# The first expert quad's products between attention's last steps

## The chip, the cores and the metric

One NeuronCore of a Trainium2 chip. The metric is the device time of one execution in microseconds (us); the kernel before took 2134.57 us (median of three runs, 2134.2 to 2135.18). TensorE is called PE, VectorE DVE, ScalarE ACT, GpSimd POOL; SP issues most DMAs. Each of these takes its instructions in the order in which the kernel issues them, and waits for the others by semaphores.

## The reference

Three layers follow each other, all in fp32:

```python
# 1 attention with random features: q, k, v are (4, 8, 576, 64), omega is (128, 64)
phi(x) = exp(x @ omega.T - |x|^2/2 - rowmax) / sqrt(128)        # x scaled by 64 ** -0.25
kv = phi(k).T @ v;  z = phi(k).sum(rows)
attn = (phi(q) @ kv) / (phi(q) @ z + 1e-6)                      # -> x: (2304, 512)
# 2 eight experts, all of them on every token; P: softmax gate, 8 rounds of row/column scaling
out = sum_e P[:, e] * (relu(x @ w1[e]) @ w2[e])                 # w1: (8, 512, 1024), w2: (8, 1024, 512)
# 3 h = out @ w_in;  y = (h - tanh(h)) @ w_out                  # 512 -> 2048 -> 512
```

## The kernel before, in words

**Attention** (to about 192 us) runs over 16 units, one for each batch and pair of heads. Iteration `i` has five steps `r` = 0 to 4; the loop (L553) runs four iterations past the last unit, and `PLAN` (L546) says which function of which unit comes in which step: in (i, r) = (17, 3) it is `num(14, 0)` and `qpT(15, 0)`. Each step begins with `flush`, which issues the ACT copies and DVE sums that the step before left in `later` and `laterv`. A unit's last stations are `zT` (PE transposes z, then DVE's row sums L472 give `den`, and POOL scales `eq` by it, L485), `qpT` (PE transposes eq into bank `qt`, L351, ACT copies it to `qp`, L502 and L507) and `num` (PE multiplies by `kz` into bank `nd`, L515, ACT copies to `xo`, L527, and SP stores it in the DRAM array `xd`, L528). All PSUM tiles come from a pool of seven banks and one for z. The attention buffers lie in pools `st` and `a2`.

**Experts.** A quad `Q` is 256 rows of the hidden layer of one expert. With tokens in four blocks, a Strassen-like scheme computes it by seven products in place of eight: `quad` (L753) issues product 0 to 7 into three banks `a`, `b`, `e` in the order a0, b1, e2, b3, a4, b5, e6; each is six matmuls (L737), since both operands are split in a high and a low fp32r part. ACT and DVE form `s1`, `u2_`, `v`, `c22` from the banks, then relu'd tiles `h`, again high (L748) and low (L751). The second product (`l2`, L846) multiplies h by w2 into banks `l`, six a quad; those of quad Q are issued within quad Q+1, two behind e2, two behind a4, and so on. In front of quad 0 stands nothing: its products begin when attention's instructions are all issued.

**Preparation** runs by generators that are moved on one step at a time. `weights` (`wprep`) loads raw weights by SP, forms four sums of blocks on POOL for each quad and splits them into seven units `u` (`split`, L82 the high part on ACT, L85 the low part on POOL), and splits w2's slabs into tiles `v`. Its jobs are in the order quad, slab, slab, quad, slab, slab; slabs need the pool `w2p`, which opens only after attention, so in attention it comes to the end of quad 0's seven units and no further. `xops` (`xprep`) loads four blocks of x from `xd`, forms three differences (L231) and splits seven units `x`; in attention's last iterations it is moved on in steps 1 and 3. In quads, `tick` (L908) after each product moves both on, and also `bg`, first the gate: it reloads x as `gx` by ACT's DMA queue, multiplies into banks `lg` and `lgT`, and then scales rows and columns.

**Taking over memory.** The pools of the expert phase (`ppm` for PSUM with five banks `q` and three `l`, `hp` for h, `tp` for the temporaries t) are opened when attention's pools are closed, at L575. A pool opened over the place of a closed one waits for the closed one's last use as a whole.

Of the kernel before, what the change touches and what calls it, by code (L numbers as in the profile page):

```python
# [19 lines left out]
def performer_moe_kernel(ctx, tc, q, k, v, omega, wg, w1, w2, win64, wout64, out):  # L20
    nc = tc.nc
# [27 lines left out]
    NU1, NU2, NV, NX = 16, 6, 7, 8  # L49

# [71 lines left out]
    def weights():  # L122
# [4 lines left out]
        for kind, s in stages:  # L127
# [134 lines left out]

    with ExitStack() as actx, tc.manual_schedule():
        pp = actx.enter_context(tc.tile_pool(name="pp", bufs=7, space=PSUM))
# [8 lines left out]
        qn = [st.tile([P, NCH, 2, D], F32, name=f"qn{i}") for i in range(2)]  # L273
        kn = [st.tile([P, NCH, 2, D], F32, name=f"kn{i}") for i in range(2)]
        vn = [st.tile([P, 2, 2, NCH, D], F32, name=f"vn{i}") for i in range(3)]
# [80 lines left out]
        def norms(u, i):  # L356
# [5 lines left out]
            tmp = a2.tile([P, NCH, 2, D], F32, tag="tmp", name=f"tmp{u}_{i}", bufs=2)  # L362
# [11 lines left out]
        def qkT(u, i):  # L374

            if ("qk", u) not in T:
                T["qk", u] = a2.tile([P, 2, S], F32, tag="qk", name=f"qk{u}")
# [16 lines left out]
        def feat(u, c):  # L394
# [13 lines left out]
            ek = a2.tile([P, 2, M], F32, tag="ek", name=f"ek{u}_{c}", bufs=7)  # L408
# [48 lines left out]
        def zT(u):  # L457

            ps = pp.tile([P, 512], F32, tag="z", name=f"z{u}", bufs=1)
# [85 lines left out]
        NORM, RED, SPL = (0, 1), (2, 4), 4  # L545
        PLAN = [  # L546
# [6 lines left out]
        for i in range(NUN + 4):  # L553
            for r, items in enumerate(PLAN):
# [4 lines left out]
                flush(feat(i, r) if i < NUN else iter(()))  # L559
                for fn, off, arg in items:  # L560
# [14 lines left out]
    ppm = ctx.enter_context(tc.tile_pool(name="ppm", bufs=5, space=PSUM))  # L575
    w2p.append(ctx.enter_context(tc.tile_pool(name="w2p", bufs=NU2)))
    accp = ctx.enter_context(tc.tile_pool(name="accp", bufs=8))
    hp_ = ctx.enter_context(tc.tile_pool(name="hp", bufs=9))
    tp = ctx.enter_context(tc.tile_pool(name="tp", bufs=2))
    phase = ExitStack()  # L580
    ctx.enter_context(tc.manual_schedule())

    def qbank(name):
        return ppm.tile([P, 512], F32, tag="q", name=name)

    def lbank(name):
        return ppm.tile([P, 512], F32, tag="l", name=name, bufs=3)

    def tmp(i, name):
        return tp.tile([P, TB], F32, tag=f"t{i}", name=name)  # L590
# [131 lines left out]
    hs = {}  # L722
    held = []
    acc = {}
    state = {"n1": 0, "x0": 0}

    FIRST = ("A", "B", "E"), ("B", "A"), ("B", "E")

    def htile(name):
        return hp_.tile([P, 2, TB], F32R, tag="h", name=name)  # L730

    def product(ps, i, start, stop, last):
        u, x = u1[state["n1"]], ux[state["x0"] + i]
        m = 0
        for wi, xi in ((0, 0), (0, 1), (1, 0)):
            for c in range(2):
                nc.tensor.matmul(  # L737
                    ps[:, :TB], u[:, wi, c], x[:, xi, c], start=(start and m == 0), stop=(stop and m == 5),
                    skip_group_check=True,
                )  # L740
                m += 1
        spent1.add(state["n1"])
        state["n1"] += 1
        if last:
            spentx.add(state["x0"] + i)

# [304 lines left out]
```

## Time and profile before

| what | us |
|---|---|
| median of three runs | 2134.57 (2134.2 to 2135.18) |
| profiled execution | 2134.26, span 2132.3, mean granted clock 0.996 |
| PE busy | 2105.9 (99% of the span), 10800 matmuls |
| DVE, POOL, ACT busy | 1783.9, 1462.0, 1051.0 |
| tail of attention, 174 to 191.88 | PE busy 14.62 of 17.88 |
| quad 0's products, 191.88 to 199.4 | PE busy 7.51 of 7.52 |
| 199.4 to 212 | PE busy 11.40 of 12.60 |
| 212 to the end | PE busy 1909.15 of 1920.30 |

A share of busy time is a mean over stages; the last four lines cut the span at the places that the change touches. A profile line of an engine gives start and duration in us, source line, operation, tile written and tiles read with their shape, the number of like instructions merged, and in brackets how long the engine stood before it and what ended that wait. The duration of a merged PE line includes the end of its last matmul, beside which the next one already runs. The granted clock is 1.00 at 2.4 GHz and 0.50 at 1.2 GHz.

### The profile page before, as it was taken

To read this page: it belongs to the slowest core of one execution; us is meant where nothing else is said; L and a number is where in the kernel's file an instruction comes from. 1 tells how busy PE (TensorE), PEld (TensorE's weight loads), DVE (VectorE), ACT (ScalarE), POOL (GpSimd) and SP (SyncE) were. 2 spreads that over 40 slices of the span, in tenths; PEclk is the share of its full clock that TensorE was granted. 3 is DMA by queue.
4 is the path that set the end of the run, shared out by engine and by line. 5 is a ranking of instruction groups with operands and counts; after the bars stand their busy time and mean duration, and the time that the engine had idled before them with its cause. 6 is when DMAs were issued, how large, how long until landed. Compare 5 with 4: busy or idle time off the path is not lost.

```text
span 2132.3 us, 33749 instructions
## 1 busy us (share of the span) xinstructions
PE 2105.9 (99%) x10800; PEld 1869.6 (88%) x10800; DVE 1783.9 (84%) x3457; ACT 1051.0 (49%) x2577; POOL 1462.0 (69%) x1981
## 2 busy tenths in 40 slices
PE   8998999999999999999999999999999999999998
PEld 6776899899998898889989899989999899989987
DVE  7885677888897798799888788788875699999997
ACT  6885333333333433333333433333333388778875
POOL 6776677767777777677777867777767546575653
PEclk9999999999999999999999999999999999999999
DMA  6444222323222333232222232323222231222220
GB/s 153 115 129 146 71 80 89 104 82 104 88 89 87 104 92 121 71 105 82 96 95 82 93 105 82 124 82 97 94 66 79 70 104 45 95 84 75 81 74 35
DMA packets 184385, 195.74 MB, mean 92 GB/s; under 512 B 53392, under 2 KB 142992, under 8 KB 184208
## 3 DMA queue, kind: packets, MB, share of 16 engines
q1 hardware_dynamic: 177200, 184.09, 27.4%
q10 hardware_dynamic: 7008, 9.51, 1.3%
q8 instruction: 85, 1.39, 0.3%
q14 instruction: 92, 0.75, 0.1%
HBM read 171.00 MB, written 22.54 MB: 91 GB/s over the span
## 4 chain that ended last, share of the span: by engine, by line
PE 75%; DVE 10%; issue 3%; ACT 2%; POOL 0%; DVEq 0%; DMA 0%; ACTq 0%; POOLq 0%
PE l L846 39%; PE b L737 14%; PE a L737 9%; PE e L737 9%; DVE t L829 3%; PE p L811 2%; DVE t L830 2%; DVE t L822 1%; DVE acc L873 1%; DVE v L85 1%; DVE x L85 1%; ACT t L828 1%; ACT u L82 0%; PE x L895 0%; DVE acc L871 0%
## 5 line engine op out<-in xcount | busy, mean ns | idle before, releaser
L846 PE MATMUL l<-v,h 128*128 128x512 f32 x4320 | 1052.4, 393 | 6.2 <-ACT h L834 3.2
L846 PEld LDWEIGHTS l<-v,h 128*128 128x128 f32 x4320 | 805.4, 188 | 164.4 <-ACT h L834 3.9
L85 POOL TENSOR_TENSOR v<-rs,v 128x256 fp32r<-128x256 f32 x432 | 334.0, 796 | 318.8 <-PE l L846 198.1
L881 DVE SCALAR_TENSOR_TENSOR acc<-l,pt,acc 128x512 f32<-128x512 f32 x516 | 380.3, 744 | 130.1 <-PE l L846 127.3
L85 POOL TENSOR_TENSOR u<-s,u 128x256 fp32r<-128x256 f32 x384 | 297.2, 785 | 81.1 <-ACT u L82 58.5
L737 PE MATMUL b<-x,u 128*128 128x384 f32 x1728 | 351.2, 338 | 0.0
L737 PEld LDWEIGHTS b<-x,u 128*128 128x128 f32 x1728 | 309.4, 188 | 15.1 <-DVE t L764 0.4
L82 ACT CAST u<-s 128x256 fp32r<-128x256 f32 x384 | 154.7, 405 | 282.8 <-POOL s L167 255.3
L737 PE MATMUL a<-x,u 128*128 128x384 f32 x1152 | 234.0, 337 | 0.9 <-ACT xo L527 0.5
L85 POOL TENSOR_TENSOR u<-rq,u 128x256 fp32r<-128x256 f32 x288 | 226.4, 786 | 12.3 <-ACT u L82 8.7
L737 PE MATMUL e<-x,u 128*128 128x384 f32 x1152 | 231.5, 335 | 0.0
L737 PEld LDWEIGHTS a<-x,u 128*128 128x128 f32 x1152 | 205.4, 188 | 10.1 <-ACT xo L527 1.5
L811 PE MATMUL p<-x,u 128*128 128x384 f32 x1152 | 212.9, 338 | 1.3 <-ACT u L82 0.7
L811 PEld LDWEIGHTS p<-x,u 128*128 128x128 f32 x1152 | 203.1, 189 | 7.5 <-POOL u L85 2.3
L737 PEld LDWEIGHTS e<-x,u 128*128 128x128 f32 x1152 | 202.8, 188 | 0.1
L835 POOL TENSOR_TENSOR h<-t,h 128x384 fp32r<-128x384 f32 x96 | 101.4, 1056 | 136.3 <-ACT h L834 129.0
L748 ACT ACTIVATE h<-b 128x384 fp32r<-128x384 f32 x96 | 47.2, 491 | 254.1 <-DVE b L786 253.3
L82 ACT CAST v<-rs 128x512 fp32r<-128x512 f32 x240 | 146.7, 621 | 40.1 <-PE l L846 38.9
L748 ACT ACTIVATE h<-t 128x384 fp32r<-128x384 f32 x96 | 50.4, 526 | 194.9 <-DVE t L773 194.9
L85 POOL TENSOR_TENSOR u<-rqi,u 128x256 fp32r<-128x256 f32 x96 | 93.8, 997 | 41.9 <-ACT u L82 39.6
L82 ACT CAST u<-rq 128x256 fp32r<-128x256 f32 x288 | 117.3, 407 | 1.6 <-ACT xo L897 1.6
L760 ACT COPY t<-a 128x384 f32<-128x384 f32 x96 | 46.1, 480 | 102.2 <-PE a L737 100.2
(141 smaller groups left out, 3071.6 us busy)
## 6 DMA issues: line engine op xcount, KB each, us to landing
rq<-in_moe_w_dram SPq DMA_DIRECT2D x96, 512.0 KB, 3.8
rs<-in_moe_w_dram SPq DMA_DIRECT2D x192, 256.0 KB, 2.8
rqi<-win SPq DMA_DIRECT2D x24, 512.0 KB, 4.6
rs<-wout SPq DMA_DIRECT2D x48, 256.0 KB, 2.8
xt<-xd SPq DMA_DIRECT2D x24, 384.0 KB, 5.9
r<-in_moe_w_in_dram SPq DMA_DIRECT2D x32, 256.0 KB, 3.2
r<-in_moe_w_out_dram SPq DMA_DIRECT2D x32, 256.0 KB, 3.5
xd<-xo SPq DMA_DIRECT2D x32, 144.0 KB, 1.8
```

Of the source, the lines that this page charges most:

```text
L82: nc.scalar.copy(dst[:, 0], src)
L85: eng.tensor_tensor(dst[:, 1, i : i + w], src[:, i : i + w], dst[:, 0, i : i + w].bitcast(F32), ALU.subtract)
L737: nc.tensor.matmul(ps[:, :TB], u[:, wi, c], x[:, xi, c], start=(start and m == 0), stop=(stop and m == 5), skip_group_check=True,)
L748: nc.scalar.activation(h[:, 0], src, AF.Relu)
L760: nc.scalar.copy(s1, A)
L811: nc.tensor.matmul(ps, u1[f + i][:, wi, c], ux[state["x0"] + 2 * t + i][:, xi, c], start=(m == 0), stop=(m == 11))
L822: nc.vector.tensor_tensor(s, u, ps, ALU.mult)
L829: nc.vector.scalar_tensor_tensor(s, gb, B1, s, ALU.add, ALU.mult)
L830: nc.vector.scalar_tensor_tensor(s, ga, A1, s, ALU.add, ALU.mult)
L835: nc.gpsimd.tensor_tensor(lo, s, hi.bitcast(F32), ALU.subtract)
L846: nc.tensor.matmul(ps, hh[f][:, hi, t : t + P], u2[n + f][:, wi], start=(f == 0 and i == 0), stop=(f == len(hh) - 1 and i == 2),)
L881: V.scalar_tensor_tensor(a, ps, p[:, e : e + 1], a, ALU.mult, ALU.add)
```

## The change

1. Product, relu, banks and temporaries (`quad`, `product`, `htile`, `tmp`, `tick`, `need`, `second`, ...) are defined ahead of attention. `quad` becomes a generator `steps` that yields after every product; `quad` runs it through.
2. Step (16, 3) closes attention's PSUM pool and two new pools `fs` and `f2` (with qn, kn, vn, qk, tmp, ek, on the right side of SBUF) and opens `ppm`, `hp` and `tp` there with `reuse_waits="tile"`: each tile then waits for what lay in its own place only. From there attention's banks are the three `l`, and z takes one `q`.
3. `DRAIN` moves quad 0 on by one product in the steps (16, 4), (17, 0) to (17, 4) and (18, 1), each behind that step's own instructions. Each product is followed by a `tick`, which here moves `wprep` on.
4. Two more steps of `xprep`, (16, 4) and (17, 2), so that each x unit is there when its product is issued.
5. Quad 1's weights come second in the jobs, ahead of the first slabs (`lead`), so that its sums and units are made in attention.
6. In the main loop quad 0 takes the ready h tiles.

```diff
+    EARLY = 1
+        lead = [k for k in range(3 * EARLY + 3) if k % 3 == 0]
+        jobs[:] = [jobs[k] for k in lead] + [j for k, j in enumerate(jobs) if k not in lead]
...
+    def open_main():
+        ppm = ctx.enter_context(tc.tile_pool(name="ppm", bufs=5, space=PSUM, reuse_waits="tile"))
+        hp = ctx.enter_context(tc.tile_pool(name="hp", bufs=9, side="right", reuse_waits="tile"))
+        tp = ctx.enter_context(tc.tile_pool(name="tp", bufs=2, side="right", reuse_waits="tile"))
+        return ppm, hp, tp
...
     def product(ps, i, start, stop, last):
+        need(state["n1"], u1, "w")
+        need(state["x0"] + i, ux, "x")
...
-    def quad(Q, last, second):
+    def steps(Q, last, second):
...
         tick()
         turn()
+        yield
...
-        second(2)
+        second(max(2, len(ready) - 6))
...
+    def early():
+        for Q in range(EARLY):
+            hh_early.append((yield from steps(Q, False, second)))
+            yield
...
         def bank(name):
-            return pp.tile([P, 512], F32, tag="b", name=name)
+            return lbank(name) if main else pp.tile([P, 512], F32, tag="b", name=name)
+        fs = units.enter_context(tc.tile_pool(name="fs", bufs=1, side="right"))
+        f2 = units.enter_context(tc.tile_pool(name="f2", bufs=2, side="right"))
...
+        DRAIN = [(0, 0, 0, 0, 1), (1, 1, 1, 1, 1), (0, 1, 0, 0, 0), (0, 0, 0, 0, 0)]
...
+                if (i, r) == (NUN, 3):
+                    units.close()
+                    main.append(open_main())
+                    begin = early()
                 for fn, off, arg in items:
...
                 if (i == 2 or i > 4) and r == SPL:
                     next(wprep, None)
-                if i > 2 * NP + 3 and r in (1, 3):
+                if i > 2 * NP + 3 and (r in (1, 3) or (i, r) in ((NUN, 4), (NUN + 1, 2))):
                     next(xprep, None)
+                if main:
+                    for _ in range(DRAIN[i - NUN][r]):
+                        next(begin, None)
...
-                hh = quad(s * NQ + Q, Q == NQ - 1, second)
-                second(len(ready))
+                if s == 0 and Q < EARLY:
+                    hh = hh_early[Q]
+                else:
...
+                    hh = quad(s * NQ + Q, Q == NQ - 1, second)
+                    second(len(ready))
```

## Rows read from the trace of the kernel before

**Rows 1.** The page's head.

```profile
span 2132.3 us, 33749 instructions
```

**Rows 2.** Busy time by stage: each engine's busy us (instructions), granted clock, DMA share, GB/s.

```profile
174.00:191.88 17.88, 14.62 (x66) 8.34 (x66) 11.70 (x55) 11.22 (x26) 9.84 (x12) 0.71 0.15 50
...
199.40:212.00 12.60, 11.40 (x73) 8.03 (x72) 3.78 (x7) 6.28 (x16) 12.52 (x20) 1.00 1.02 358
212.00:2132.30 1920.30, 1909.15 (x9567) 1717.99 (x9565) 1615.71 (x2750) 897.90 (x2092) 1317.74 (x1661) 1.00 0.27 87
```

**Rows 3.** The same in half microseconds around the fall and rise of the clock.

```profile
181.00:181.50 0.50, 0.50 (x6) 0.50 (x4) 0.41 (x3) 0.07 (x1) 0.00 (x0) 0.56 0.00 0
...
191.00:191.50 0.50, 0.35 (x2) 0.00 (x0) 0.50 (x2) 0.20 (x2) 0.00 (x0) 0.70 0.00 0
```

**Rows 4.** Timeline of PE, tail of attention: start, us, operation, idle before and its releaser.

```profile
176.95 0.71 PE L515 MATMUL nd<-qp,kz 128*64 128x288 f32 x4
...
179.05 0.32 PE L351 MATMUL qt<-ident,eq 112*128 112x112 f32 x1 [0.97 <-POOL eq L485]
...
180.51 0.44 PE L462 MATMUL z<-ident,zr 128*128 128x128 f32 x2
...
187.50 1.41 PE L351 MATMUL qt<-ident,eq 128*128 128x128 f32 x6
...
191.88 1.31 PE L737 MATMUL a<-x,u 128*128 128x384 f32 x6 [0.53 <-ACT xo L527]
...
198.23 1.20 PE L737 MATMUL e<-x,u 128*128 128x384 f32 x6
```

**Rows 5.** Timeline of ACT, same stretch.

```profile
180.03 0.55 ACT L502 COPY qp<-qt 128x464 f32<-128x464 f32 x1 [1.88 <-PE qt L351]
...
191.43 0.40 ACT L527 COPY xo<-nd 128x288 f32<-128x288 f32 x1 [0.30 <-ACT xo L527]
193.74 0.48 ACT L760 COPY t<-a 128x384 f32<-128x384 f32 x1 [1.91 <-DMA xd<-xo]
...
199.44 0.41 ACT L82 CAST u<-s 128x256 fp32r<-128x256 f32 x1 [0.71 <-POOL s L167]
```

**Rows 6.** Timeline of DVE, same stretch.

```profile
177.28 1.25 DVE L231 TENSOR_TENSOR xt<-xt,xt 128x768 f32<-128x768 f32 x1
...
178.85 0.28 DVE L451 TENSOR_SCALAR kz<-kv 128x128 f32<-128x128 f32 x1
...
181.09 0.29 DVE L472 CUSTOM_DVE_ANT_0 jk<-eq,z 128x128 f32<-128x128 f32 x1 [0.71 <-PE z L462]
...
194.33 0.56 DVE L764 TENSOR_TENSOR t<-b,t 128x384 f32<-128x384 f32 x1 [2.37 <-PE b L737]
```

**Rows 7.** Timeline of POOL, two windows.

```profile
166.44 1.77 POOL L485 TENSOR_TENSOR eq<-eq,den 128x256 f32<-128x256 f32 x3 [2.23 <-DVE nm L412]
...
176.53 4.33 POOL L485 TENSOR_TENSOR eq<-eq,den 128x256 f32<-128x256 f32 x5 [6.18 <-DVE den L472]
182.87 3.61 POOL L485 TENSOR_TENSOR eq<-eq,den 128x256 f32<-128x256 f32 x5 [2.02 <-DVE den L472]
186.44 1.95 POOL L85 TENSOR_TENSOR x<-xt,x 128x384 fp32r<-128x384 f32 x2
194.87 2.83 POOL L85 TENSOR_TENSOR v<-rs,v 128x256 fp32r<-128x256 f32 x4 [6.48 <-ACT v L82]
...
200.78 0.72 POOL L85 TENSOR_TENSOR u<-rq,u 128x256 fp32r<-128x256 f32 x1
```

**Rows 8.** Timeline of PE behind quad 0.

```profile
205.79 1.55 PE L846 MATMUL l<-v,h 128*128 128x512 f32 x6
208.13 0.85 PE L623 MATMUL lg<-gx,wgr 128*32 128x384 f32 x8 [0.78 <-DVE acc L871]
```

**Rows 9.** DMA issues from 140 to 216: KB each, median us to landing.

```profile
gx<-xd ACTq DMA_DIRECT2D x12, 384.0 KB, 5.1
...
rq<-in_moe_w_dram SPq DMA_DIRECT2D x2, 512.0 KB, 6.2
```

More of the change, by code (lines that the diff above doesn't have):

```diff
@@ L260, in ready_x, with qbank @@
         return (kind, s) in xdone
+    main, hh_early = [], []
+    def open_main():
[3 more added lines that the diff above has]
+        return ppm, hp, tp
+    def qbank(name):
+        return main[0][0].tile([P, 512], F32, tag="q", name=name)
@@ new lines, in lbank, with tmp, htile, product @@
+    def lbank(name):
+        return main[0][0].tile([P, 512], F32, tag="l", name=name, bufs=3)
+    def tmp(i, name):
+        return main[0][2].tile([P, TB], F32, tag=f"t{i}", name=name)
+    hs = {}
+    held = []
+    acc = {}
+    state = {"n1": 0, "x0": 0}
+    FIRST = ("A", "B", "E"), ("B", "A"), ("B", "E")
+    def htile(name):
+        return main[0][1].tile([P, 2, TB], F32R, tag="h", name=name)
+    def product(ps, i, start, stop, last):
+        need(state["n1"], u1, "w")
+        need(state["x0"] + i, ux, "x")
+        u, x = u1[state["n1"]], ux[state["x0"] + i]
+        m = 0
+        for wi, xi in ((0, 0), (0, 1), (1, 0)):
+            for c in range(2):
+                nc.tensor.matmul(
+                    ps[:, :TB], u[:, wi, c], x[:, xi, c], start=(start and m == 0), stop=(stop and m == 5),
+                    skip_group_check=True,
+                )
+                m += 1
+        spent1.add(state["n1"])
+        state["n1"] += 1
+        if last:
+            spentx.add(state["x0"] + i)
@@ new lines, in performer_moe_kernel, with tick, need @@
+    bg = []
+    pace = [0, 1, False, False]
+    def tick():
+        next(wprep, None)
+        pace[0] += 1
+        if pace[3] or pace[0] % 8 == 0:
+            next(xprep, None)
+        if bg and not pace[2] and (pace[1] == 1 or pace[0] * 12 % 32 < 12):
+            try:
+                next(bg[0])
+            except StopIteration:
+                bg.pop(0)
+    def need(n, have, what):
+        k = 0
+        while n not in have:
+            k += 1
+            assert k < 1000, what
+            next(wprep if what == "w" else xprep)
@@ L263, in performer_moe_kernel, with turn, second @@
+    turned = []
+    def turn():
+        if turned:
+            turned.pop(0)()
+    ready, begun = [], {}
+    def second(n):
+        for _ in range(n):
+            if ready:
+                ready.pop(0)()
+                tick()
+    def early():
+        for Q in range(EARLY):
+            hh_early.append((yield from steps(Q, False, second)))
+            yield
     with ExitStack() as actx, tc.manual_schedule():
-        pp = actx.enter_context(tc.tile_pool(name="pp", bufs=7, space=PSUM))
+        units = ExitStack()
+        pp = units.enter_context(tc.tile_pool(name="pp", bufs=7, space=PSUM))
@@ L272, in performer_moe_kernel @@
         bd = st.tile([P, 2 * M], F32, name="bd")
[L273 to L275 removed]
+        qn = [fs.tile([P, NCH, 2, D], F32, name=f"qn{i}") for i in range(2)]
+        kn = [fs.tile([P, NCH, 2, D], F32, name=f"kn{i}") for i in range(2)]
+        vn = [fs.tile([P, 2, 2, NCH, D], F32, name=f"vn{i}") for i in range(3)]
@@ L719, in convert @@
         converted.append(True)
[L722 to L745, printed above, removed]
@@ L901, in x2 @@
             xdone.add((1, s))
-    bg = []
-    pace = [0, 1, False, True]
-    def tick():
-        next(wprep, None)
-        pace[0] += 1
-        if pace[3] or pace[0] % 8 == 0:
-            next(xprep, None)
-        if bg and not pace[2] and (pace[1] == 1 or pace[0] * 12 % 32 < 12):
-            try:
-                next(bg[0])
-            except StopIteration:
-                bg.pop(0)
-    def need(n, have, what):
-        k = 0
-        while n not in have:
-            k += 1
-            assert k < 1000, what
-            next(wprep if what == "w" else xprep)
-    turned = []
-    def turn():
-        if turned:
-            turned.pop(0)()
     gtp = phase.enter_context(tc.tile_pool(name="gtp", bufs=1))
@@ L935, in performer_moe_kernel @@
     bg.append(gate(gtp))
-    ready, begun = [], {}
-    def second(n):
-        for _ in range(n):
-            if ready:
-                ready.pop(0)()
-                tick()
     n2 = 0
```

136 lines of the change are left out of this document (70 added, 66 removed).

## The prediction, made before the changed kernel ran

> **What bounds the kernel now.** I read first the windows by stage. From 212 us to the end PE is busy 1909 of 1920 us [rows 2]: whatever reaches 212 us earlier arrives earlier by as much, and only the stretch before is worth reading. In the tail of attention (174 to 191.88) PE stands 3.3 us and its mean granted clock is 0.71; from 199.4 to 212 it stands 1.2 us. The half-microsecond windows place the clock: PE stands from 178.1 to 179.05, the clock falls to 1.2 GHz at 181.1 (mean 0.56 in that half) and is back at 2.4 GHz at 191.3 (mean 0.70), 3.8 us into a gapless run of PE from 187.5 [rows 3, 4]. Ten us at half clock are 5 us of PE lost. Last, the timelines of the engines: the tail is a chain DVE sums, POOL scaling of eq, PE transposes (qt), ACT copies, PE products (nd), and PE follows it [rows 4 to 7]. So some 9.5 us (3.3 + 1.2 + 5) are what any reordering could win here at most.
>
> **The change part by part.** The 42 matmuls of quad 0 stand from 191.88 to 199.37 now, 7.49 us, 1.04 to 1.07 a product (I use 1.04, the step from start to start) [rows 4]. They move behind (16,4) to (18,1); nothing is removed. With them move their ACT copies and relus, their DVE sums, the last units of x, and the preparation of quad 1's seven units (ACT cast 0.41, POOL 0.72 each) out of the stretch after 200 us. Everything is issued in the written order, so I lay each engine's queue out from 180.66, where z of the last unit ends; until there nothing on the chain moves (quad 1's four sums on POOL fall into its idle times ahead of eq, 2.2 us and 6.2 us [rows 7]).
>
> *PE's work.* Left of attention: nine groups worth 4.3 us at full clock (four nd at 0.62, which is 0.71 less the overlap with the next; transposes 0.46 a half, 0.22 a rest, estimates at half the durations that the qt rows show at half clock) [rows 4]. With 7 x 1.04 = 7.3 that is 11.6 us. Clock: the fall at 181.1 has its reason before, so it stays. It rose after 3.8 us without a gap; with products behind (14,1) PE is gapless from 180.5, so I put the rise at 184.5, a loss of 1.7 us. Without any wait PE would be through at 180.66 + 11.6 + 1.7 = 194.0.
>
> *What the queues add.* ACT: qp ends 180.6 [rows 5]; then u7's cast 0.41 and x3's 0.79 (twice as many elements as the cast of a u, an estimate), to 181.8, then the copy s1, which waits for product a0 (6 matmuls at half clock, 181.1 to 183.1) and holds everything behind it: 183.7; u8 184.2; xo and qp of unit 14, 185.0; u9 185.4; qp's rest 185.6; x4's cast 186.4. DVE: x3's low part, 181.6 to 182.6 (1.0; 1.25 for the subtraction of the same shape at 177.28, beside POOL), now stands ahead of the last sums, which ran at 181.09 and let POOL begin eq at 182.87: 1.5 us, to 184.1; then u2 (0.56), which waits for b1 until 185.3, and only then the rest of the sums, to 186.9 [rows 6]. POOL: u8 184.2 to 184.95, three eq by 0.72 (3.61 for five) to 187.1, u9 187.8, two eq to 189.2 (the first of them 188.6), and x4's low part, 2 x 0.97 [rows 7], at 190.2 and 191.2. PE: a0 183.1, rest of (14,2) 183.6, b1 185.1, e2 186.2, b3 187.2, nd 187.8; the transposes of unit 15 wait for eq until 188.6 (0.5 lost); a4 can run two matmuls, then waits for the halves of x4 (1.2 and 0.8 lost): 191.8; nd 192.4; the next transposes need a bank of only three that ACT empties behind a4's relu (0.8 lost): 193.7; b5, rest, e6 196.0; two nd 197.2. So quad 0 and attention together end at about 197.2, against 199.37 with quad 0 last: 2.2 gained, 3.3 us of waits eaten.
>
> *What is late next.* The weights of the second product, v0 and v1, are still taken from the space of the pool that closes with attention: the first ACT instruction behind it waited 1.91 us for the last xd<-xo, until 193.66, 2.2 after that xo started [rows 5]. With xo at 197.6 this is 199.8; v0's cast (0.65, the time from ACT's copy to POOL's first half of v) and POOL's halves (2.83 us for the four of v0 and v1 [rows 5, 7]) give v0 at 202.0 and v1 at 203.5. Quad 1's a, b, e need neither (u7 to u13 are ready at 194.9) and run 197.2 to 200.4; then l of quad 0 waits 1.8 for v0 and 0.7 for v1 and ends at 204.3. Before, the same l ended at 207.34 (205.79 + 1.55), with two lg groups and one lgT done as well, 0.78 each (0.85 less overlap) [rows 8], which come later in the new order. 204.3 + 2.3 = 206.6, against 207.3: 0.8 gained. The 0.78 us that lg waited at 208.13 for a bank [rows 8] I count half, 0.4, since lg now starts one step later among the l's. **Sum: -1.2 us.** gx (5.1 to land, issued at about 202) and quad 2's weights (6.2, issued at about 202.5; [rows 9]) then reach their users, lg at 207.7 and quad 2 at some 218, in time. POOL then has v2, v3, four sums and seven units, some 11 us, for quad 2: covered by PE's 14 us of quad 1 and l's; if that cover were gone it would cost the difference, under 3 us.
>
> *Bounds of the terms.* Clock: never fallen (0.8 more gained, because the waits for POOL remain) to low until 191.3 as before, whatever runs (0.8 less; some of its cost lies beside the waits). Waits of 3.3: from 0 (all of it hidden) to 6, if POOL's instructions take what eq took at 176.53, 4.33 for five, rather than 1.77 for three at 166.44 [rows 7]. The stall on v0 and v1, 2.5: from 0 (if quad 1's further products stood there) to 4. The new places: each waits for what lay there last, at most for kz at 179.13 instead of nd's start at 176.95 [rows 4, 6], of which the wait for eq behind it swallows all but 0.9; I take 0, since kz's end is the latest of all and only one of eight places can be its bank.
>
> Of POOL the rows show 0.59 us for an eq at 166.44 and 0.87 at 176.53, where DVE ran a subtraction of two SBUF tiles meanwhile [rows 6, 7]. The Trainium skill, page "SBUF — State Buffer", section "Who interferes with whom", says that DVE with two SBUF inputs and POOL lock each other out. That speaks against the change, which puts three low parts of x on DVE and seven units on POOL into the chain; it is rival C.
>
> **The rivals.**
> A, the chain hides it all: quad 0 fills only what PE lost anyway. Waits of 3.3 gone, quad and attention end at 194.0, the mark comes 3.2 earlier, and the wait of 0.78 goes whole: -1.2 - 3.2 - 0.4 = -4.8, 2129.8. For it: the 3.3 us idle and the slow clock [rows 2]. Against: ACT, DVE and POOL are in order, and each has a piece of quad 0 ahead of a piece of the chain.
> B, the new places wait for the whole closed pools (the change does not do what it says): all first uses wait for 179.13; 0.9 on the chain: -0.3, 2134.3. Against: the pools' last readers are done before the tail's critical part.
> C, POOL is held by DVE: 20% on POOL's times of this stretch (a choice between none and 0.87/0.59 = 1.47), with the queues laid out again, moves the mark by 3.2: +2.0, 2136.6. For: 0.87 against 0.59. Against: 182.87's 0.72, with little of DVE beside it, is in the sum already.
> D, slower, the clock falls a second time: place, the wait for v0 and v1 (200.4 to 203.5), where PE has 0.7 us of work; before the fall at 181.1 its longest stand was 0.97 [rows 4]. Price: as long at half clock as from 181.1 to 191.3, 10 us, 5 lost: +3.8, 2138.4; with a return as quick as the forecast's, +0.6. It decides whether the clock falls in that wait as it fell behind the 0.97. Against: products run densely on both sides, and the clock held through the 1.2 us that PE stood from 199.4 to 212 [rows 2].
>
> **How the numbers follow.** The profiled execution took 2134.26 (span 2132.3 and 2.0 around it) [rows 1], 0.3 below the median 2134.57; the gain is taken off the median: 2134.57 - 1.2 = 2133.4. Chances: forecast 0.42 (its own range 2131.5 to 2135.5), A 0.22, B 0.06, C 0.12, D 0.18. A change under 0.2% (4.3 us, so 2130.3 to 2138.8) cannot be told from none by a measurement of this kernel. Faster: most of A (0.17) and the forecast's lower edge (0.05), 0.22. Slower: the half of D on which C's 2.0 come as well (2140.4; 0.10) and 0.03 of C, 0.13. Same: 0.65. The range leaves out the lower part of A and the upper half of D: 2128.4 to 2138.4.
>
> **What would show it.** In the changed kernel: products a to e among nd and qt from 181 to 196; DVE's sums (L472's successor) starting at about 182.6 instead of 181.09; PE's product a4 waiting for POOL's x; quad 1's first product right behind the last nd; l waiting for POOL's v at some 200 to 203.5; the mark (end of the first l) at 203.5 to 205. Wrong if the last nd comes before 195 (A) or after 199.5 (C), if the clock has a second low stretch after 200 (D), or if the first uses of the new banks wait at 177 (B); and wrong in its frame if PE loses time after 212, where it was gapless.

## The result: slower by 0.66%, most of it after the stretch that the prediction worked out

The changed kernel took 2148.07 us (median of 6 runs, 2142.66 to 2150.24) against 2133.99 for the kernel before beside it (6 runs, 2127.61 to 2135.18): a ratio of 1.0066, 95% interval 1.0049 to 1.0083. The forecast was 2133.4, its range 2128.4 to 2138.4; the time lies above it. The executions of either kernel differ by up to 7.6 us, so medians are compared; a trace shows one execution. The profiled execution took 2148.71, span 2146.9, 14.6 longer than the span before [rows 1].

The windows by stage of the changed kernel, answering to [rows 2] (per engine busy us and instructions; then clock and DMA):

```profile
174.00:200.00 26.00, 21.66 (x113) 16.66 (x115) 18.19 (x63) 15.64 (x40) 15.84 (x19) 0.87 0.11 36
200.00:212.00 12.00, 9.38 (x33) 6.59 (x32) 3.38 (x6) 3.07 (x7) 4.16 (x6) 0.72 0.65 206
212.00:2146.90 1934.90, 1924.27 (x9602) 1716.06 (x9601) 1618.34 (x2750) 900.09 (x2098) 1322.31 (x1668) 1.00 0.27 88
```

After 212 PE stands no more than before (10.6 us against 11.2 [rows 2]), yet the stretch is 14.6 us longer, for 35 matmuls more. The window 500 to 1000 us, in the middle of the long stage, shows why. First the kernel before, then the changed one:

```profile
500.00:1000.00 500.00, 499.92 (x2502) 450.03 (x2501) 428.63 (x749) 191.71 (x460) 364.62 (x479) 1.00 0.30 94
```

```profile
500.00:1000.00 500.00, 499.54 (x2484) 446.25 (x2483) 426.53 (x742) 190.04 (x456) 361.47 (x475) 1.00 0.30 95
```

Same clock (1.00, 2.4 GHz), PE busy throughout, and 18 matmuls fewer. A busy engine can be slow: here the count tells it, and the busy share does not. The first stage's end in PE's timelines (start, duration), before and after:

```profile
1703.79 2.22 PE L846 MATMUL l<-v,h 128*128 128x512 f32 x9
1705.85 2.27 PE L811 MATMUL p<-x,u 128*128 128x384 f32 x12
```

```profile
1717.63 2.96 PE L923 MATMUL l<-v,h 128*128 128x512 f32 x12
1720.44 2.26 PE L888 MATMUL p<-x,u 128*128 128x384 f32 x12
```

The first p is 14.59 later. I set every PE matmul of the changed kernel beside the same one of before. Its lag ("shift") is -0.36 us until 165, +0.91 at 172, -1.43 at the last l of quad 0, the 36th l (before at 226.33), +4.92 at the last l of quad 1, the 72nd (242.81), +14.59 at the first p (1705.85), +14.90 at the last p (2107.04). So some 5 us are lost early, 9.7 evenly between 243 and 1706, nothing after.

The **step** of a matmul is the time from its start to the start of the next on PE; I take the mean between 500 and 1500 us, without the few steps over 250 ns. Of l it is 230.1 ns before and 233.4 after; of a, b and e 175.5, 176.2, 173.5 and 175.0, 175.4, 173.6. The first stage has 3456 l, 1152 a, 1728 b and 1152 e: 3456 x 3.33 - 1152 x 0.48 - 1728 x 0.87 + 1152 x 0.08 = 9.5 us, which is the even loss.

**The early part.** PE's timeline of the changed kernel, for [rows 4, 8]:

```profile
182.02 1.30 PE L300 MATMUL a<-x,u 128*128 128x384 f32 x6
185.45 0.68 PE L300 MATMUL a<-x,u 128*128 128x384 f32 x3
188.34 0.60 PE L300 MATMUL a<-x,u 128*128 128x384 f32 x2
190.49 0.59 PE L300 MATMUL a<-x,u 128*128 128x384 f32 x1 [1.56 <-POOL x L86]
191.45 1.33 PE L300 MATMUL a<-x,u 128*128 128x384 f32 x3 [0.37 <-POOL x L86]
199.84 1.19 PE L676 MATMUL nd<-qp,kz 128*64 128x288 f32 x8
201.24 1.21 PE L300 MATMUL e<-x,u 128*128 128x384 f32 x6
204.38 0.79 PE L923 MATMUL l<-v,h 128*128 128x512 f32 x1 [1.93 <-ACT v L83]
205.87 5.15 PE L923 MATMUL l<-v,h 128*128 128x512 f32 x11 [0.69 <-POOL v L86]
226.08 0.85 PE L781 MATMUL lg<-gx,wgr 128*32 128x384 f32 x8 [0.78 <-DVE acc L948]
```

Quad 0 stands among attention's steps, a4 waits for POOL's x, and l waits for v, as forecast. Not forecast: the three matmuls of a at 185.45. Quad 0's own a are the six at 182.02 and the 2 + 1 + 3 from 188.34, so these three are of quad 1's first product. PE's order is not the written one, unlike what the opening section says: matmuls written behind attention run among its last steps. Whether they are moved when the program is built or by the engine no run here shows. Windows of half a us of the changed kernel, for [rows 3]:

```profile
181.00:181.50 0.50, 0.50 (x5) 0.09 (x2) 0.29 (x1) 0.50 (x2) 0.50 (x1) 1.00 0.00 0
190.50:191.00 0.50, 0.50 (x1) 0.18 (x1) 0.50 (x2) 0.26 (x1) 0.50 (x1) 0.63 0.00 0
197.00:197.50 0.50, 0.50 (x5) 0.50 (x4) 0.00 (x0) 0.00 (x0) 0.00 (x0) 0.54 0.04 9
204.00:204.50 0.50, 0.12 (x1) 0.12 (x1) 0.00 (x0) 0.50 (x2) 0.10 (x1) 0.79 0.00 0
211.00:211.50 0.50, 0.50 (x5) 0.50 (x4) 0.44 (x1) 0.00 (x0) 0.00 (x0) 0.89 1.07 385
```

The clock no longer falls at 181. It falls behind a4's stand, to 197.5, and again behind the stand for v, to 211: two stretches of 6.8 us at 1.2 GHz in place of one of 10.2 [rows 3]. Where it falls differs between executions: in e14's (below), the same order with v moved by 32 bytes, the clock is low around 182 to 185 too, and again later:

```profile
182.00:185.00 3.00, 3.00 (x13) 2.14 (x14) 1.74 (x7) 1.58 (x3) 1.60 (x2) 0.50 0.00 0
196.00:198.00 2.00, 2.00 (x9) 1.90 (x8) 0.09 (x1) 0.83 (x3) 1.60 (x3) 0.50 0.41 136
206.00:212.00 6.00, 5.25 (x12) 3.63 (x12) 0.69 (x1) 0.74 (x2) 3.84 (x6) 0.50 0.94 295
```

What holds ACT and POOL, for [rows 5, 7]:

```profile
203.71 0.62 ACT L83 CAST v<-rs 128x512 fp32r<-128x512 f32 x1 [2.08 <-DMA xd<-xo]
211.77 0.62 ACT L83 CAST v<-rs 128x512 fp32r<-128x512 f32 x1 [5.42 <-DMA rs<-in_moe_w_dram]
213.39 0.52 ACT L311 ACTIVATE h<-t 128x384 fp32r<-128x384 f32 x1 [1.00 <-DVE t L347]
188.73 2.67 POOL L86 TENSOR_TENSOR x<-xt,x 128x384 fp32r<-128x384 f32 x2
```

The fourth slab's cast waited 5.42 us on ACT for its load, and quad 1's relu stood behind it; in the kernel before seven u of quad 1 lie between the second slab and the third. PE did not pay for this wait here. From that cast to the last l of quad 1 it stands 0.88 us, 0.78 of it the wait at 226.08, which the kernel before has at 208.13 [rows 8]:

```profile
211.77:247.73 35.96, 35.08 (x209) 26.55 (x208) 16.18 (x29) 13.75 (x33) 20.69 (x30) 1.00 0.50 162
```

Nor does the rise of the shift from -1.43 to +4.92 say so. At the last l of quad 0 the changed kernel has still to run 24 lg and 24 lgT that the kernel before has done by then, some 5.1 us of PE (0.78 for eight lg, 0.69 for six lgT).

The early loss adds up ahead of 212. From 165 us to the last l of quad 1 PE stands 9.4 us in place of 5.7 (stands over 0.06 us): 1.2 more up to z, 1.93 at a4 and 2.62 at the first l, less 2.2 that the kernel before stands from 183 to 202. At 1.2 GHz half of PE's busy time is lost: 6.3 us in place of 4.5. Together that is 5.4 us more, against 5.3 measured (from -0.36 to +4.92).

### The profile page after: what moved, and what is told of

It reads as the page before. It is cut to its first block, busy times and chain, and to the rows that moved or that the text cites. A ratio compares the mean times of both kernels' runs of the same rounds, so it can differ in the third digit from the quotient of the medians.

```text
span 2146.9 us, 33744 instructions
## 1 busy us (share of the span) xinstructions
PE 2118.3 (99%) x10800; PEld 1867.1 (87%) x10800; DVE 1790.2 (83%) x3457; ACT 1050.7 (49%) x2577; POOL 1462.6 (68%) x1981
## 4 chain that ended last, share of the span: by engine, by line
PE 87%; DVE 8%; issue 2%; ACT 2%; POOL 0%; DMA 0%; SPq 0%; DVEq 0%; ACTq 0%; POOLq 0%
PE l L923 43%; PE b L300 14%; PE a L300 9%; PE e L300 9%; PE p L888 6%; PE pr L561 2%; DVE t L906 1%; PE kv L592 1%; DVE t L907 1%; DVE t L899 1%; PE nd L676 1%; DVE mx L571 1%; DVE acc L950 1%; PE qt L512 1%; DVE jk L633 1%
## 5 line engine op out<-in xcount | busy, mean ns | idle before, releaser
L923 PE MATMUL l<-v,h 128*128 128x512 f32 x4320 | 1070.9, 397 | 8.3 <-ACT h L911 2.6
L86 POOL TENSOR_TENSOR u<-rq,u 128x256 fp32r<-128x256 f32 x288 | 226.6, 787 | 12.0 <-ACT u L83 10.2
L888 PE MATMUL p<-x,u 128*128 128x384 f32 x1152 | 210.8, 337 | 0.4 <-ACT u L83 0.4
```

The source lines that it names most:

```text
L86: eng.tensor_tensor(dst[:, 1, i : i + w], src[:, i : i + w], dst[:, 0, i : i + w].bitcast(F32), ALU.subtract)
L888: nc.tensor.matmul(ps, u1[f + i][:, wi, c], ux[state["x0"] + 2 * t + i][:, xi, c], start=(m == 0), stop=(m == 11))
L923: nc.tensor.matmul(ps, hh[f][:, hi, t : t + P], u2[n + f][:, wi], start=(f == 0 and i == 0), stop=(f == len(hh) - 1 and i == 2),)
```

## The experiments

All times are medians, ratios against the kernel before run beside them, with 95% intervals. "Place" of h or v is where their tiles start in a partition, in bytes past a multiple of 256; the tiles' pitch is a multiple of 256. Before: h 0, v 0. Changed: h 224 (the pool moved to the right side of SBUF), v 0. In both, u and x are at 0.

### Placement or banks: e1, e2, e3, e4

**e1**, the kernel before with h moved:

```diff
+    pad1 = ctx.enter_context(tc.tile_pool(name="pad1", bufs=1)).tile([P, 8], F32, name="pad1")
     hp_ = ctx.enter_context(tc.tile_pool(name="hp", bufs=9))
+    pad2 = ctx.enter_context(tc.tile_pool(name="pad2", bufs=1)).tile([P, 8], F32, name="pad2")
...
```

> The kernel before, with the nine h tiles alone moved up by 32 bytes (a 32-byte tile ahead of them and one behind, so that the temporaries move by 64); h then starts 32 bytes past a multiple of 64, as in the changed kernel. In the changed kernel the steps from one l matmul to the next are 234.2 ns against 230.8 (500 to 1500 us), and 9.5 of the 14.6 us come in evenly over the l matmuls of the first expert stage. T1 (h's address decides, by its offset): l steps of 233.5 to 234.5 ns and 9 to 12 us more than before, 2143 to 2146. T2 (the banks of l decide): 230.8 ns and no change within 1 us. T3 (which h tile is read beside which v, or h lying 22 KB higher, decides): 230.8 ns, no change.

2139.27, 1.0030 [1.0019, 1.0041]. Step of l 233.2; in its trace the shift grows from +0.7 to +9.7 over the first stage. In the trace 32 bytes of padding bring 9.0 of the 9.7 us of even loss into the kernel before. The medians differ by 5.7 us, less than the 9 to 12 of T1; so too in e4 and e7, where the traces show 9 us over the first stage and the medians 6. Why they differ is open. The two pads also move the temporaries t by 64 bytes; e13 against e7 moves h alone.

**e2**, the kernel before with l in banks 0 to 2, as in the changed one:

```diff
+    nc.vector.memset(lbank("l2")[:, :8], 0.0)
```

> The kernel before, with one l bank taken first, so that l lies in banks 0 to 2 and the products in 3 to 7, as in the changed kernel; one small memset is added. T1 (h's offset): 230.8 ns between l matmuls and no change within 1 us. T2 (banks): 233.5 to 234.5 ns, 9 to 12 us slower. T3: no change.

2131.19, 0.9995 [0.9985, 1.0005], step 230.1: the banks make no difference here.

**e3**, the changed kernel with h back at a multiple of 256:

```diff
+    padr = ctx.enter_context(tc.tile_pool(name="padr", bufs=1, side="right")).tile([P, 56], F32, name="padr")
```

> The changed kernel, with a tile of 224 bytes at the right end of SBUF, so that h (and everything else there) starts at a multiple of 256, as in the kernel before; banks, order and pairing as in the changed kernel. T1 (h's offset): l steps back to 229 to 232 ns, 8 to 11 us less than the changed kernel; what stays over the kernel before is the 5 us that the trace shows ahead of 260 us (3.4 us of PE standing, 1.7 us of half clock). T2 (banks) or T3 (place or pairing): 234 ns, as the changed kernel.

2136.5, 1.0014 [1.0005, 1.0023], step 230.1. The shift is -0.3 before the tail, +3.4 at the last l of quad 1 and +4.2 at the first p: the even loss is gone, and most of the early one stays (3.8 of 5.3). With h back in its place the changed kernel lies inside the forecast's range.

**e4**, the changed kernel without quad 0's products in attention (`DRAIN` moves nothing):

```diff
-    EARLY = 1
+    EARLY = 0
```

> The changed kernel with no quad issued early (EARLY = 0): the takeover of banks and buffers in step (16, 3), the two more steps of x and h's new place stay; quad 0 and quad 1's weights come after attention as before. If the early products cost the 5 us ahead of 260 us and the placement the 9.5 us after it: 9 to 11 us slower than before, with the clock falling once at about 181 and PE standing no more than before. If instead the takeover itself costs the early time (waits of its first tiles): 14 us slower, as the whole change.

2139.36, 1.0027 [1.0016, 1.0037], step 233.4: the shift is -0.6 before the tail, -1.6 at the 72nd l and +7.3 at the first p. The early loss belongs to the early products and what goes with them, the even loss to h's place. Nothing is lost by the taking over itself.

### Which place: e5, e6, e7

**e5**, before with h tiles 32 bytes longer, so that nine tiles stand at 0, 32, ... 224, 0; **e6**, before with u moved by 32 bytes; **e7**, before with v moved by 32 bytes:

```diff
-        return hp_.tile([P, 2, TB], F32R, tag="h", name=name)
+        t = hp_.tile([P, 2 * TB + 8], F32R, tag="h", name=name)
+        return t[:, : 2 * TB].rearrange("p (a t) -> p a t", a=2)
```

```diff
+    pads = [ctx.enter_context(tc.tile_pool(name="pad1", bufs=1)).tile([P, 8], F32, name="pad1")]
     w1p = ctx.enter_context(tc.tile_pool(name="w1p", bufs=NU1))
```

```diff
+    pads = [ctx.enter_context(tc.tile_pool(name="pad1", bufs=1)).tile([P, 8], F32, name="pad1")]
     w2p.append(ctx.enter_context(tc.tile_pool(name="w2p", bufs=NU2)))
+    pads.append(ctx.enter_context(tc.tile_pool(name="pad2", bufs=1)).tile([P, 56], F32, name="pad2"))
```

> The kernel before, with each of the nine h tiles 32 bytes longer, so that they start at offsets 0, 32, 64, ... 224, 0 within 256 bytes. T1a (what counts is that h starts at a multiple of 64): steps between l matmuls as before on the tiles at 0, 64, 128, 192, and 233 to 235 ns on the odd ones, mean about 231.5 ns, 4 to 6 us slower. T1b (only multiples of 256 are good): mean about 233 ns, 8 to 10 us slower. T1c (32 past is bad only as the constant offset of all tiles against v): mean at or under 230 ns.

> The kernel before, with the sixteen tiles u (the stationary operand of the products, as h is of l) 32 bytes past a multiple of 64, everything behind them again at a multiple of 256. T1 as a rule for any stationary operand: the products' steps, 172 to 176 ns, grow by 2 to 4 ns; 5184 products of the first stage and 1152 of the second then cost 10 to 20 us. If it is only of l (512 columns, near the limit of what the engine streams): no change of the products and none of the time.

> The kernel before, with the six tiles v (the moving operand of l) 32 bytes past a multiple of 64 and h at a multiple of 256. If the offset matters for the stationary operand only: l steps 230 ns, no change. If it is the relation of h to v that matters (both off would be good, one off bad): 233 to 234 ns, 9 to 11 us slower. If any operand that starts off a multiple of 64 costs: likewise slower, so this run and e5 have to be read together.

e5: 2133.5, 1.0007 [0.9998, 1.0016], step of l 231.3, between the two; 1.1 us more than before, where T1a said 4 to 6. e6: 2131.93, 0.9995 [0.9986, 1.0004]; l 230.4, and a and b faster (174.1 and 173.8 from 175.5 and 176.2). e7: 2138.76, 1.0027 [1.0015, 1.0039], step 233.1. So h is not special: v moved alone costs as much. Moving u, the first product's h, costs nothing, so T1 as a rule for any stationary operand is out.

### Both operands: e9, e13

**e9**, before with h and v (and acc between them) 32 bytes further; **e13** the same with acc back at 0:

```diff
+    pads = [ctx.enter_context(tc.tile_pool(name="pad1", bufs=1)).tile([P, 8], F32, name="pad1")]
     w2p.append(ctx.enter_context(tc.tile_pool(name="w2p", bufs=NU2)))
...
     hp_ = ctx.enter_context(tc.tile_pool(name="hp", bufs=9))
+    pads.append(ctx.enter_context(tc.tile_pool(name="pad2", bufs=1)).tile([P, 56], F32, name="pad2"))
```

```diff
+    pads.append(ctx.enter_context(tc.tile_pool(name="pad2", bufs=1)).tile([P, 56], F32, name="pad2"))
     accp = ctx.enter_context(tc.tile_pool(name="accp", bufs=8))
+    pads.append(ctx.enter_context(tc.tile_pool(name="pad3", bufs=1)).tile([P, 8], F32, name="pad3"))
     hp_ = ctx.enter_context(tc.tile_pool(name="hp", bufs=9))
+    pads.append(ctx.enter_context(tc.tile_pool(name="pad4", bufs=1)).tile([P, 56], F32, name="pad4"))
...
```

> The kernel before with its h tiles and its v tiles both 32 bytes further (each alone made the step of the second product's matmul 233.1 to 233.2 ns from 230.1, and the time 5 to 6 us longer). Theory T1a, each operand's own place counts: the step stays at 233 ns if one misplaced operand is enough (time about 2138, +5 to +6) or goes to 236 if the two add (+18 in the trace, about 2145). Rival T1r, only the difference of the two places counts: 230.1 ns and no change of time.

> e9_both_shift32 moved h and v by 32 bytes, and acc too; it was 0.67% faster than before, which neither theory had said: the step of the second product's matmul fell to 227.6 ns, a and b of the first product to 173.7. Here h and v are moved by 32 and acc stays at a multiple of 256. Theory T1r', the pair of h and v makes the step and 32 with 32 is better than 0 with 0: 227.6 ns and 173.7, time about 2121. Rival A, the gain is acc's (VectorE's reads and writes of it beside the matmuls): 230.1 ns, time as before, 2133.

e9: 2120.97, 0.9933 [0.9917, 0.9948]; e13: 2119.13, 0.9937 [0.9923, 0.9952]. Both miss what T1a and T1r said, and e13 comes out as T1r' said: l's step is 227.6, under that of before, and a and b go to 173.6 and 173.7. The window of e13 has 21 matmuls more than before in the same 500 us:

```profile
500.00:1000.00 500.00, 499.49 (x2523) 452.15 (x2523) 430.89 (x756) 192.65 (x463) 369.49 (x484) 1.00 0.30 95
```

acc is out. Between e7 and e13 only h is moved, and the step falls from 233.1 to 227.6: what counts is how h and v stand to each other, and 0 with 0 is not the best.

One rival can be read off the traces: that the other engines' reads and writes make the long step. In the changed kernel the step from l to l is 233.2 to 233.7 ns whichever of DVE, ACT and POOL run beside it, in e13 226.8 to 227.2; in e7 the 16 steps with none of them beside have 233.3. So that is out. But a matmul's own two operands are not the whole either. The products a and b read neither h nor v, and their steps go with them: of the six matmuls of a b the fourth and sixth are the long ones before (181.2 and 178.9 ns), the first and third in the changed kernel (177.6 and 179.0), and none in e13 (173.4 to 174.5).

### The changed kernel's places: e14, e16, e17, e18

**e14**, the changed kernel with v alone moved by 32 (as in e7); **e16**, its taking over without `DRAIN`'s products (`EARLY = 0` as in e4), v so moved, and the slabs' pool taken over place by place; **e17** and **e18**, e16 with h 192 and 64 bytes lower:

```diff
-    w2p.append(ctx.enter_context(tc.tile_pool(name="w2p", bufs=NU2)))
+    pads = [ctx.enter_context(tc.tile_pool(name="pad1", bufs=1)).tile([P, 8], F32, name="pad1")]
+    w2p.append(ctx.enter_context(tc.tile_pool(name="w2p", bufs=NU2, reuse_waits="tile")))
...
```

```diff
+    padr = ctx.enter_context(tc.tile_pool(name="padr", bufs=1, side="right")).tile([P, 48], F32, name="padr")
```

> The changed kernel as it is, with the v tiles alone 32 bytes further, so that v stands as h does in it. Theory T1r': step 233.4 -> 227.6 ns and products at 173.4; of the change's loss only the early 5 us stay, less some 14: time about 2125, faster than both. Rival T1a' (h at the place that the change gave it is bad by itself, on the right side of SBUF or beside other neighbours): 233 ns or more, time 2145 or more. Rival A (acc makes e9's gain): 230, time about 2138.

> Taking over place by place, the slabs' pool too, no early products, h where the change put it and v moved by 32 bytes. By T1r' and e12's early gain of 4 us (its first l's): 2117 to 2119, and against e15 it tells whether mended early products are worth anything beside it (theory: nothing, within 2 us). By A about 2130.

> e16_takeover_both32 with h 192 bytes lower: h and v then stand both 32 past a multiple of 256, as in e9 and e13 (step 227.6 ns there, 229.66 in e16, where h stood 224 past one and v 32). Theory P, h must stand where v does within the multiple: 227.6 ns, 7 us less than e16, about 2114, faster than every kernel so far. Rival R, what lowers the step to 227.6 needs h on the left side of SBUF, behind acc: 229.7 ns, time as e16, 2121.

> e16_takeover_both32 with h 64 bytes lower: 160 past a multiple of 256, so 32 past one of 128, with v 32 past one of 256. Theory P128, the places are counted modulo 128 bytes: as e17, 227.6 ns, 2114. Rival P256, modulo 256 or more: other than e17, 229 to 230 ns, 2120 or so. By R as e16.

| kernel | place of h, v | step of l, ns | us | ratio |
|---|---|---|---|---|
| before | 0, 0 | 230.1 | | |
| changed | 224, 0 | 233.4 | 2148.07 | 1.0066 [1.0049, 1.0083] |
| e1 | 32, 0 | 233.2 | 2139.27 | 1.0030 [1.0019, 1.0041] |
| e7 | 0, 32 | 233.1 | 2138.76 | 1.0027 [1.0015, 1.0039] |
| e13 | 32, 32 | 227.6 | 2119.13 | 0.9937 [0.9923, 0.9952] |
| e14 | 224, 32 | 229.7 | 2130.31 | 0.9991 [0.9982, 1.0000] |
| e16 | 224, 32 | 229.7 | 2120.73 | 0.9945 [0.9933, 0.9958] |
| e17 | 32, 32 | 227.6 | 2116.20 | 0.9924 [0.9911, 0.9937] |
| e18 | 160, 32 | 231.6 | 2128.34 | 0.9981 [0.9972, 0.9990] |

e14: moving only v takes the changed kernel from 2148 to 2130, with its early loss still in it (shift +6.1 at the 72nd l, -0.2 at the 3456th). It missed 227.6, and e17 says why: with h at 32 as v is, on the same side of SBUF, the step is 227.6 as in e9 and e13. e18, equal modulo 128 but not 256, has 231.6: P128 and R are out, and P256 is right only in that it differs (229 to 230 was said). e18's longer l is made up by shorter a and b: its shift is -2.2 at the 72nd l and -2.3 at the first p. e16 (2117 to 2119 said) and e17 (2114 said) came out some 2 us longer. e17 is the fastest of all, 0.76% under the kernel before, and here are its window of the middle and its line of the page:

```profile
500.00:1000.00 500.00, 499.55 (x2524) 452.39 (x2523) 431.43 (x756) 193.00 (x466) 368.98 (x483) 1.00 0.30 95
```

```profile
L929 PE MATMUL l<-v,h 128*128 128x512 f32 x4320 | 1043.5, 391 | 7.1 <-ACT h L917 3.8
```

The same line of the page has 1052.4 us and 393 ns before; 2 ns in the mean of 4320 is what all this looks like there.

### The early loss: e8, e10, e11, e12, e15

**e8**, e3 with two stands mended: the low part of a4's x on DVE, and no l behind e2 of quad 1:

```diff
-                unit(b[key], G if kind and m % 2 or not kind and m == 4 else V)
+                unit(b[key], G if kind and m % 2 or not kind and s and m == 4 else V)
...
-        second(max(2, len(ready) - 6))
+        if Q != EARLY:
+            second(2)
```

> The changed kernel with h at a multiple of 256 (as e3), with x4 of the first token block split by DVE in place of POOL, and without the two l groups that quad 1 issues behind e2 (they come later in the quad), so that neither a4 waits for x nor l for v. If the early loss is these two waits and the clock that falls in them (3.4 us of standing and 1.7 of half clock in the changed kernel): PE's stands from 174 to 226 shrink by 3 us or more, at most one fall of the clock, and 2 to 6 us less than before: 2128 to 2132 where before is 2133.6. If the early products hold up the chain whatever waits: 2134 to 2137, as e3.

2134.88, 1.0010 [0.9999, 1.0022]: the clock stays at 1.00 to 212, but from a start of +1.5 the shift is still +3.7 at the 72nd l. By the time it fell into the second range that was said, as e3; by the shift 1.6 us of e3's 3.8 are gone. Its rows show the next wait: the cast of the fourth slab, DVE behind the relu that stands behind it, and the quad's l, whose bank waits for DVE. Here, unlike in the changed kernel, the slab costs PE 1.99 us, and then the clock falls (212 to 217: 0.66):

```profile
209.41 0.62 ACT L83 CAST v<-rs 128x512 fp32r<-128x512 f32 x1 [5.12 <-DMA rs<-in_moe_w_dram]
210.49 0.76 DVE L314 SCALAR_TENSOR_TENSOR h<-t,h 128x384 fp32r<-128x384 f32 x1 [8.07 <-ACT h L311]
212.37 2.55 PE L926 MATMUL l<-v,h 128*128 128x512 f32 x6 [1.99 <-DVE acc L951]
```

**e11** mends these: slabs three and four behind quad 2's units, the slabs' pool taken over place by place (`reuse_waits="tile"` as in e16, not printed here):

```diff
-        lead = [k for k in range(3 * EARLY + 3) if k % 3 == 0]
-        jobs[:] = [jobs[k] for k in lead] + [j for k, j in enumerate(jobs) if k not in lead]
+        order = [0, 3, 1, 2, 6, 4, 5, 9, 7, 8, 10, 12, 11, 13, 14]
+        jobs[:15] = [jobs[k] for k in order]
```

> e8_early_mended with two edits: the second slab pair is prepared behind quad 2's units and not directly behind the first pair, and the slabs' pool also takes over place by place. Theory S, what the early products still lose after 200 us is ACT held by slabs: 2.1 us for the last store of xo and 5.1 us for the load of the fourth slab, with relu and gate copies behind it. Then PE's stands between 202 and 224 us (1.4 + 2.0 + 0.8 + 0.8) fall to under 2, the 72nd l is at the attention's shift minus 2 to plus 0, and the time is 0 to 3 us under the kernel before. Rival B, the loads themselves are late whatever the order (the queues carry gx and weights for 25 us behind attention, and quad 0's products stood beside them before): the stands move to lg or to quad 2's products, the 72nd l stays 2 us or more behind, the time at or above that of before.

2131.78, 0.9994 [0.9985, 1.0002]. Quad 0's l run without a stand, the casts of v follow the last xo:

```profile
200.15 3.02 PE L926 MATMUL l<-v,h 128*128 128x512 f32 x12
197.46 0.64 ACT L83 CAST v<-rs 128x512 fp32r<-128x512 f32 x1
```

From -0.4 before the tail the shift is -4.3 at the 72nd l: theory S, and the early products now gain 3.9 us. Which of e11's two edits does how much is not taken apart. But the taking over without early products gains nearly as much. **e10** is e3 with `EARLY = 0`; **e12** is e10 with the slabs' pool taken over place by place and u 32 bytes further (the lines of e16 and e6):

> The changed kernel without early products (quad 0 stands behind attention as before) and with the h tiles at multiples of 256 bytes: the taking over of banks and places is all that is left. Theory T2, the loss of the change is the h tiles' place (9 us) and the early products (5 us), and nothing else: step of the second product's matmul 230.1 ns, PE's first l's 1 to 2 us earlier than before and no drift after; time 0 to 2 us under the kernel before, not to be told from it. Rival T3, the new pools cost something of their own: drift over the first stage with a step over 231 ns, time +3 or more.

> e10_takeover_aligned with the slabs' pool taking over place by place and the first product's weight tiles u 32 bytes further (in e6 the products' steps went from 175.7 to 174.3 and from 176.5 to 174.1 ns with it, 3.7 us over the first stage). Theory U, these gains are real and add: PE 1.5 to 3 us early at the first l's and a drift of minus 3 more, time 2129, 4 us under the kernel before. Rival N, what e6 showed belongs to that one run: steps and time as e10.

e10: 2130.4, 0.9989 [0.9979, 0.9999], shift -0.8 before the tail and -2.1 at the 72nd l, flat after. e12: 2126.39, 0.9967 [0.9954, 0.9979], -1.0 and -4.2, and then -7.9 at the first p, with e6's steps of a and b (174.1 and 173.8): theory U. My expectation of e10 said that quad 0 stands behind attention there; its rows say otherwise:

```profile
180.51 0.60 PE L300 MATMUL a<-x,u 128*128 128x384 f32 x2
181.04 0.97 PE L678 MATMUL nd<-qp,kz 128*64 128x288 f32 x4
181.94 0.96 PE L300 MATMUL a<-x,u 128*128 128x384 f32 x4
182.74 1.20 PE L300 MATMUL b<-x,u 128*128 128x384 f32 x6
```

Once the places are free early, a0, b1 and e2 are taken ahead among attention's last steps without being written there; PE fills with work whose inputs are ready. What the traces show it to win is the clock, which in e10 does not fall in the tail (0.80 in this window before):

```profile
174.00:200.00 26.00, 20.87 (x119) 14.25 (x118) 18.14 (x62) 15.68 (x38) 17.80 (x22) 1.00 0.40 130
```

In the traces of the eight kernels without the taking over (before, e1, e2, e5, e6, e7, e9, e13) the tail has 6.8 to 13.7 us at 1.2 GHz. In the six with it and without `DRAIN`'s products (e4, e10, e12, e16, e17, e18) it has none or 3.4. In the six with the early products (changed, e3, e8, e11, e14, e15) the stretch up to 217 has 3.4 to 13.7.

**e15** is e11 with h at 224 and v at 32, as in e16:

> e11_early_slabs (early products mended, 2131.8) with h left where the change put it and v moved by 32 bytes. By T1r' step 227.6 ns and 12 to 14 us less than e11: about 2119. By A no change from e11.

2123.69, 0.9959 [0.9948, 0.9971], step of l 229.7 as in e14 and e16 and not 227.6, 8 us less than e11 and not 12 to 14. e16 beside it took 2120.73. From before the tail to the 72nd l e15 gains 3.4 us (+0.5 to -2.9), e16 3.4 (-1.7 to -5.1). These are single executions, with 6.8 us of low clock in e15's tail and none in e16's; by the medians e15 is 3.0 us longer. Mended, `DRAIN`'s early products are worth nothing beside the taking over.

## Why the prediction was wrong

**The step that failed** is the frame and one term in it: "whatever reaches 212 us earlier arrives earlier by as much, and only the stretch before is worth reading", and "The new places: each waits for what lay there last [...] I take 0". I priced new places as waits alone, bounded them by 0.9, and took l's step as given. h's place made it 3.3 ns longer, 9.5 us net of what a and b gained, shown by e1 (put into the kernel before) and e3 (taken out of the changed one, which then takes 2136.5, inside the range). The text did name the sign, "wrong in its frame if PE loses time after 212", but looked for it as idle time, and PE is not idle.

**The early term**, forecast -1.2, measured +5.3 (from -0.36 to +4.92); e4 shows that it comes with the early products. The step in it that failed is the clock: forecast 1.7 us lost, measured 6.3, which is 4.6 of the 6.5 between forecast and measurement. By its steps:

- That up to 180.66 "nothing on the chain moves" was wrong by 1.25 us. Quad 1's sums stand in POOL's gaps, but where POOL goes from eq straight on to them (169.2 to 171.4), DVE's `nb`, on which ACT's next exponentials wait, took 1.53 us and not 0.27. The jump of 1.25 stands in every trace with quad 1's weights moved ahead and in none with `EARLY = 0`; no run moves the sums alone. DVE's timeline of the kernel before, then of the changed one, then POOL's of the changed one:

```profile
168.74 0.27 DVE L414 TENSOR_TENSOR nb<-nm,sq 112x4 f32<-112x4 f32 x1 [0.46 <-DVE nm L412]
```

```profile
168.39 1.53 DVE L575 TENSOR_TENSOR nb<-nm,sq 112x4 f32<-112x4 f32 x1 [0.46 <-DVE nm L573]
```

```profile
168.03 1.18 POOL L646 TENSOR_TENSOR eq<-eq,den 112x256 f32<-112x256 f32 x2 [0.17 <-DVE nm L573]
169.17 0.73 POOL L172 TENSOR_TENSOR s<-rq 128x256 f32<-128x256 f32 x1
169.86 1.51 POOL L173 TENSOR_TENSOR s<-rq,s 128x256 f32<-128x256 f32 x1
```

- The two larger waits were right in place and size: a4 stood 1.56 + 0.37 (forecast 1.2 + 0.8), the first l 1.93 + 0.69 (1.8 + 0.7). The 0.5 and 0.8 forecast ahead of two groups of transposes did not come. POOL's x took 2.67 against the 1.95 of [rows 7], while DVE made another x in 2.34, forecast as 1.0: rival C's contention, in rows of this stretch.

```profile
187.24 2.34 DVE L86 TENSOR_TENSOR x<-xt,x 128x768 fp32r<-128x768 f32 x1 [0.70 <-ACT x L83]
```

- The Trainium skill, page "SBUF — State Buffer", section "Who interferes with whom", calls the port pair that DVE and POOL share an exclusive lock. 2.67, 2.34 and 1.53 agree in that instructions of both are longer where they meet.
- The clock was wrong both ways: in this execution it did not fall at 181 (in e14's it did), and it fell behind a4's stand and behind the stand for v. The second is rival D, and its point of decision was named rightly: the clock is low behind that stand in the changed kernel and in e14, and the first twelve l of quad 0 took from 204.4 to 210.8. D's price by the quick return, +0.6, is +0.5 by the forecast's own 1.7.
- "What is late next" counted v2 and v3 as POOL's work, covered by quad 1, and left out their loads. With quad 1's units moved ahead of the first slabs, four slabs follow each other, and the fourth's cast stood 5.42 us on ACT ahead of quad 1's relus. In the changed kernel PE was late already and stood only 0.88 us behind it; once the earlier waits are mended (e8) it stands 1.99 there. e11, which mends this together with the slabs' pool, is where the shift turns to -4.3.
- The order of PE was taken as written. It is not, and in e10 the taking over with h aligned gains 1.3 us up to the 72nd l, as much as `DRAIN` was to give.
- One reading is off by 0.3 us: z of the last unit ends at 180.95 (180.51 + 0.44 in [rows 4]) and not at 180.66. It decides nothing.

Rival A came about only in e11, with h aligned and four edits to the early products and the slabs (its -4.8 against -3.9 measured from the attention's shift). Rival B did not come: no first use of a new bank waits at 177.

## What to carry to other kernels

When a change moves buffers, compare the count of matmuls in one full window of the steady stage before anything else: an engine at 99% can lose 0.7% without a single idle us. Try the operands' start modulo 256 bytes as a tuning parameter of its own (here 14 us of 2133 by places alone in e13, 17 with the taking over in e17, against nothing for the reordering by hand). Moving work ahead needs every queue behind it read again, loads and casts that now stand back to back among them. Before a lag is read off one matmul, count the work that lies behind it in both kernels.

## What was not expected of the hardware

- The mean step of the 128x512 matmuls l, in a stretch where PE is busy throughout, goes with the starts of their two SBUF operands (h, v): 227.6 ns (32, 32), 229.7 (224, 32), 230.1 (0, 0), 231.6 (160, 32), 233.1 to 233.4 (one of them 32 off). The Trainium skill, page "SBUF — State Buffer", section "Who interferes with whom", gives PE separate and independent ports for the moving operand and for weight loads, and says that only the port pair of DVE and POOL causes contention. That gives no reason for these steps: moving v alone and moving h alone cost the same, and moving both gains. Which rule makes them is open: neither each start nor the difference alone does, u moved by 32 shortens a and b by 1.4 and 2.4 ns, and a and b go with h and v, which they do not read.
- The bank of l (0 to 2 or 5 to 7) makes no difference: 230.1 ns in both.
